# Transposing q and k by DMA instead of on TensorE, and score tiles in triples, in a fused attention and MLP kernel

## The chip, the cores and the metric

The kernel runs on one core of a Trainium2 chip. The metric is the device time of one execution in microseconds. The kernel before takes 482.68 us (median of 3 runs, 482.49 to 484.44).

## The reference, cut to what matters

```python
q_n, k_n = rmsnorm(q, g_q), rmsnorm(k, g_k)          # (8 batches, 12 heads, 448, 64)
scores = (1 / 8) * q_n @ k_n.T                       # per head
attn = softmax(scores); x = attn @ v                 # -> (3584, 768)
h = x @ w_in                                         # 768 -> 2048
out = (max(h, 0) + alpha * min(h, 0)) @ w_out        # 2048 -> 768
```

Inputs and output are float32; the kernel computes in float16 with float32 accumulation.

## The kernel before

Work goes by groups of four heads, three groups to a batch, 24 in all (numbered from 0). A group's q and k are loaded, squared (GpSimd), summed (DVE), given a reciprocal root (ACT) and scaled (GpSimd). Fourteen TensorE transposes, seven for q and seven for k, put them into PSUM, and DVE copies them out; the copy of k multiplies in both gains, so g_q and g_k enter there together. Scores are made in tiles: four 64x64 matmuls each, seven tiles to a group. An exponential on ACT follows. A group's denominators and value products are 28 matmuls each. The MLP of the batch before (128 up-projections, 56 down-projections in all) fills the gaps between bursts of score tiles.

```python
def turn(y):                                  # per group
    ps = psa.tile([128, 2, 512], FP32, name="tps", tag="acc")
    ...
    for tp, nm in zip(tps, "qk"):
        for j in range(J):                    # J = 7
            nc.tensor.transpose(tp[:, j, :], qs[y, nm][:, j]..., ident)
    for tp, nm in zip(tps, "qk"):
        t = att.tile([128, 2, J, 64], FP16, name=f"{nm}T", tag=f"{nm}T", bufs=3)
        if nm == "q": nc.vector.tensor_copy(out=o, in_=i4)
        else: nc.vector.tensor_scalar(out=o, in0=i4, scalar1=gain[:, 0:1], ..., op0=ALU.mult)
...
dens = {last(y) + 1: y for y in range(NG)}    # burst at which group y's denominators run
avs = {last(y) + 2: y for y in range(NG)}
...
for b in range(1, B):
    at(J * G * b / 2 - 4, load_v, b)          # v of batch 1 at burst 6
...
for c in range(4):
    load_w_in(c)                              # float32 -> float16, GpSimd's queue
    at(8 + 2 * c, load_w_out, c)
...
for n in range(NB + 2):                       # a burst: two score tiles
    ...
```

Of the kernel before, what the change touches and what calls it, by code (L numbers as in the profile page):

```python
# [21 lines left out]
def kernel(  # L22
# [51 lines left out]
    make_identity(nc, ident)  # L74
    idle = cst.tile([128, S], FP16, name="idle", tag="idle")
    nc.vector.memset(idle, 0.0)
    gain = cst.tile([128, 1], FP32, name="gain", tag="gain")
    gk2 = cst.tile([128, 1], FP32, name="gk2", tag="gk2")
    alpha_sb = cst.tile([128, NF], FP32, name="alpha_sb", tag="alpha_sb")
    w_in_sb = cst.tile([128, KM, DF], FP16, name="w_in_sb", tag="w_in_sb")  # L80
    w_out_sb = cst.tile([128, NF, DM], FP16, name="w_out_sb", tag="w_out_sb")
    gT = cst.tile([128, NF, W], FP16, name="gT", tag="gT")
# [2 lines left out]
    SRC = {"q": q4, "k": k4}  # L85


    def load_qk(y):
        b, i = divmod(y, G)
        for nm in "qk":  # L90
            t = ld.tile([128, 2, J, D], FP32, name="nat", tag="nat", bufs=6)
            for g in range(2):
                (nc.scalar if y < 2 and g else nc.sync).dma_start(
                    out=t[ds(64 * g, 64)].rearrange("p h j d -> p h (j d)"),
                    in_=SRC[nm][b, g, :, ds(2 * i, 2)],
                )
            nat[y, nm] = t
# [21 lines left out]

    def square(y, nm):  # L120
        src = nat[y, nm].rearrange("p h j d -> p (h j d)")
        sq = ld.tile([128, 2 * J, D], FP32, name="sq", tag="sq", bufs=2)
        sqf = sq.rearrange("p n d -> p (n d)")
        if y < 2:
            nc.scalar.activation(out=sqf, in_=src, func=AF.Square)  # L125
        else:
            nc.gpsimd.tensor_mul(out=sqf, in0=src, in1=src)  # L127
        sqs[y, nm] = sq
# [18 lines left out]
    def scale(y, nm):  # L147
# [6 lines left out]
        )  # L154
        qs[y, nm] = t

    def turn(y):

        ps = psa.tile([128, 2, 512], FP32, name="tps", tag="acc")
        tps = [  # L160
            ps[:, n, : S].bitcast(FP16).rearrange("p (j c) -> p j c", j=J)
            for n in range(2)
        ]
        for tp, nm in zip(tps, "qk"):
            for j in range(J):
                nc.tensor.transpose(  # L166
                    tp[:, j, :], qs[y, nm][:, j].rearrange("p h d -> p (h d)"), ident
                )
        for tp, nm in zip(tps, "qk"):
            t = att.tile([128, 2, J, 64], FP16, name=f"{nm}T", tag=f"{nm}T", bufs=3)  # L170
            o = t.rearrange("p g j c -> p j g c")
            i4 = tp.rearrange("p j (g c) -> p j g c", g=2)
            if nm == "q":
                nc.vector.tensor_copy(out=o, in_=i4)
            else:
                nc.vector.tensor_scalar(  # L176
                    out=o, in0=i4, scalar1=gain[:, 0:1], scalar2=None, op0=ALU.mult
                )
            qkT[y, nm] = t

# [3 lines left out]
    def score(y, j):  # L184
        qT, kT = qkT[y, "q"], qkT[y, "k"]
        sc = pss.tile([128, 2, 512], FP32, name="sc", tag="sc")
        for par in range(2):
            for g in range(2):
                nc.tensor.matmul(  # L189
                    out=sc[ds(64 * g, 64), par, :S],  # L190
                    lhsT=kT[ds(64 * par, 64), g, j, :],
                    rhs=qT[ds(64 * par, 64), g].rearrange("p j c -> p (j c)"),
                    start=True,
                    stop=True,
                )
        scs[y, j] = sc
# [33 lines left out]
    def invert(y):  # L230
        r = rden[y]
        nc.scalar.activation(out=r, in_=r, func=AF.Exp, scale=-1.0)  # L232
# [60 lines left out]



    NB = (NG * J + 1) // 2

    def last(y):
        return (J * y + J - 1) // 2

    dens = {last(y) + 1: y for y in range(NG)}
    avs = {last(y) + 2: y for y in range(NG)}
    prep, post, roots = {}, {}, {}

    def at(n, f, *a):
        prep.setdefault(max(int(n), 0), []).append((f, a))
# [1 line left out]
    def after(n, f, *a):  # L308
        post.setdefault(max(int(n), 0), []).append((f, a))

    turn_at = [J * y // 2 - 1 for y in range(NG)]
    turns = {n: y for y, n in enumerate(turn_at) if y}
    jobs = {}
    for y in range(G, NG):

        n = turn_at[y - 1] if y < G + 2 else last(y - G) + 2
        at(n - 8, load_qk, y)
        for nm in "qk":
            at(n - 2, square, y, nm)
            if y < G + 2:  # L320
                after(n, reduce, y, nm)
            else:
                jobs.setdefault(n, []).append((reduce, (y, nm)))
        roots[n + 1] = y
    for b in range(1, B):
        at(J * G * b / 2 - 4, load_v, b)


    UP, DOWN = 1.13, 2.6
# [2 lines left out]
    for b in range(B):  # L332
        ups = [(UP, up, (b, ft)) for ft in range(NF)]
        odd = b % 2
        new = [
            (DOWN, down, (b - odd, t, oh))
            for t in (range(3, J) if odd else range(3)) for oh in range(2)
        ]
        tail = len(new) if b == B - 1 else 2 + odd
        periods.append((ups, carry, new[:tail]))  # L340
        carry = new[tail:]

    def cost(n):
        return 0.75 + (1.35 if n in dens or n in avs else 0.0) + (0.9 if n in turns else 0.0)

    first = last(G - 1) + 2
    gaps = [[] for _ in range(NB + 2)]
    for b in range(B - 1):
        lo = last(G * b + G - 1) + 2
        hi = last(G * b + 2 * G - 1) + 2  # L350
        ups, old, new = (list(u) for u in periods[b])
        mlp = sum(u[0] for u in ups + old + new)
        per = (mlp + sum(cost(n) for n in range(lo, hi))) / (hi - lo)
        clock = 0.0
        for n in range(lo, hi):
            clock += cost(n)
            free = n in avs or n in turns
            while ups or old or new:
                if old and (free or not ups):
                    u = old.pop(0)  # L360
                elif ups:
                    u = ups.pop(0)
                else:
                    u = new.pop(0)
                gaps[n].append(u[1:])
                clock += u[0]
                free = False
                ahead = 0.5 * (UP if ups else DOWN)
                if n < hi - 1 and clock + ahead > per * (n - lo + 1):
                    break  # L370
    ups, old, new = periods[B - 1]
    rest = []
# [6 lines left out]

    load_qk(0)  # L380
    nc.scalar.preload_act_table_set("natural_log_exp_and_others")
    for g in range(2):
        nc.gpsimd.dma_start(out=gain[ds(64 * g, 64)], in_=g_q.unsqueeze(1))
        nc.gpsimd.dma_start(out=gk2[ds(64 * g, 64)], in_=g_k.unsqueeze(1))
    load_qk(1)
    load_qk(2)
    nc.sync.dma_start(out=alpha_sb, in_=moe_alpha.rearrange("(t p) -> p t", p=128))

    spin(34)
    for nm in "qk":  # L390
        square(0, nm)
        reduce(0, nm)
    for nm in "qk":
        root(0, nm)
        scale(0, nm)
    nc.vector.tensor_mul(out=gain, in0=gain, in1=gk2)
    turn(0)
    load_v(0)
    for y in (1, 2):
# [3 lines left out]
                reduce(y, nm)  # L403
    for c in range(4):
        load_w_in(c)
        at(8 + 2 * c, load_w_out, c)
    after(0, root, 1)
    for nm in "qk":
        after(0, scale, 1, nm)
        after(2, reduce, 2, nm)  # L410
    roots[3] = 2

    for n in range(NB + 2):
        for f, a in prep.get(n, ()):
            f(*a)
        tiles = [divmod(m, J) for m in (2 * n, 2 * n + 1) if m < NG * J]
        for t in tiles:
            score(*t)
        if n in dens:
            den(dens[n])  # L420
        if n in avs:
            attv(avs[n])

        plain = n not in dens and n not in avs and n not in turns
        wait = plain and gaps[n] and gaps[n][0][0] is up
        late = []
        for t in tiles[:1] if wait else tiles:
            soft(*t)
        if wait:
            late = [(1, soft, t) for t in tiles[1:]]  # L430
        if n in dens:
            log(dens[n])
            late = [(2, invert, (dens[n],))]
        if n in roots:
            y = roots[n]
            root(y)
            for nm in "qk":
                scale(y, nm)
        if n in turns:
            turn(turns[n])  # L440
        done = 0
        for f, a in gaps[n]:
            if f is down:
                down(*a, jobs.pop(n, ()))
            else:
                f(*a)
                done += 1
                if late and done == late[0][0]:
                    for _, g, c in late:
                        g(*c)  # L450
                    late = []
        for _, g, c in late:
            g(*c)
        if n < first:
            spin(4 if plain else 1)
        for f, a in jobs.pop(n, []) + post.get(n, []):
            f(*a)
    for f, a in rest:
# [31 lines left out]
```

## Time and profile before

| stretch (us) | PE busy | ACT | DVE | GpSimd | DMA engines |
|---|---|---|---|---|---|
| 40 to 65 | 21.1 of 25 | 20.5 | 12.2 | 17.0 | full |
| 65 to 100 | 33.5 of 35 | 25.2 | 19.4 | 15.9 | 0.56 |
| 100 to 400 | 292.0 of 300 | 192.2 | 141.3 | 107.8 | 0.33 |

From 100 us on PE has hardly anything left to wait for: time there is PE work. Up to the first up-projection PE runs idle matmuls to keep its clock up, and the end of the opening is set by loads, GpSimd, ACT and DVE. The prediction below shows the lines for both. It puts the first up-projection at 50.7 us; that is its third matmul. The first two stand at 49.39, and the third then waited 0.78 us for xT. Times of the first up-projection in the rest of this document are those of its first matmul, 49.39 before.

### The profile page before, as it was taken

What the parts mean: (1) busy time and instruction counts of PE and PEld (TensorE: products, weight loads), DVE (VectorE), ACT (ScalarE), POOL (GpSimd) and SP (SyncE); (2) the same over time, 40 slices, a digit from 0 to 9 for tenths busy, and PEclk for the clock granted to TensorE, in tenths of its full rate; (3) what the DMA queues carried; (4) which work ended last, traced back from release to release, by engine and by line L of the source; (5) the groups of instructions that cost most, each with busy time, mean ns of one, the idle gap of its engine ahead of it and who ended that gap; (6) DMA issues with size and microseconds to landing.
All of it is one profiled execution on the core that took longest, in us unless ns stands there. A gap on an engine that the chain in (4) does not pass through costs nothing.

```text
span 480.6 us, 9494 instructions
## 1 busy us (share of the span) xinstructions
PE 451.2 (94%) x4074; PEld 234.9 (49%) x4074; DVE 217.3 (45%) x312; ACT 289.1 (60%) x399; POOL 167.0 (35%) x123
## 2 busy tenths in 40 slices
PE   7777899999999999999999999999999999999995
PEld 3243444555455445555545554554545554555463
DVE  2843564545354445355453454454462443334421
ACT  4788789567756657656755757548674558423300
POOL 4688734554253261451442351532623200000000
PEclk9799999999999999999999999999999999999998
DMA  7999997340705243431704434423401110111122
GB/s 197 200 266 221 241 209 135 110 110 3 167 1 143 77 116 53 117 100 38 167 0 110 110 100 69 110 54 90 92 1 35 34 34 1 34 34 33 34 65 67
DMA packets 32187, 45.46 MB, mean 95 GB/s; under 512 B 5008, under 2 KB 28560, under 8 KB 32144
## 3 DMA queue, kind: packets, MB, share of 16 engines
q1 hardware_dynamic: 19792, 32.13, 25.8%
q0 software_dynamic: 11776, 11.80, 15.7%
q10 hardware_dynamic: 576, 0.92, 0.7%
q8 instruction: 32, 0.52, 0.5%
q14 instruction: 11, 0.09, 0.1%
HBM read 45.62 MB, written 11.01 MB: 118 GB/s over the span
## 4 chain that ended last, share of the span: by engine, by line
PE 70%; ACT 12%; DVE 9%; issue 4%; POOL 3%; DMA 1%; SPq 0%; POOLq 0%; DVEq 0%; ACTq 0%
PE op L266 30%; PE hT L249 20%; ACT ah L257 6%; PE sc L189 6%; PE av L212 6%; PE dn L212 4%; DVE gT L258 4%; ACT expT L201 4%; DVE ss L133 3%; PE tps L166 2%; DMA nat<-in_k_dram 1%; POOL qs L150 1%; POOL sq L127 1%; ACT rden L227 1%; PE spin L289 1%
## 5 line engine op out<-in xcount | busy, mean ns | idle before, releaser
L201 ACT ACTIVATE expT<-sc,expb 128x896 f16<-128x896 f32 x168 | 160.4, 1004 | 51.2 <-PE sc L189 51.1
L249 PE MATMUL hT<-xT,w_in_sb 128*128 128x448 f16 x768 | 159.9, 352 | 8.1 <-DVE gT L258 6.5
L266 PE MATMUL op<-w_out_sb,gT 128*128 128x384 f16 x896 | 153.3, 326 | 1.7 <-DVE gT L258 1.7
L257 ACT ACTIVATE ah<-hT,alpha_sb 128x448 f16<-128x448 f32 x128 | 80.7, 635 | 97.2 <-PE hT L249 96.2
L258 DVE TENSOR_TENSOR gT<-hT,ah 128x448 f16<-128x448 f32 x128 | 79.5, 624 | 123.5 <-ACT ah L257 123.3
L150 POOL TENSOR_TENSOR qs<-nat,rr 128x896 f16<-128x896 f32 x45 | 75.0, 1688 | 127.9 <-ACT rr L145 104.1
L266 PEld LDWEIGHTS <-gT 128*128 128x128 f16 x896 | 85.2, 98 | 64.3 <-issue 11.2
L249 PEld LDWEIGHTS <-w_in_sb 128*128 128x128 f16 x768 | 72.4, 97 | 86.0 <-issue 26.2
L127 POOL TENSOR_TENSOR sq<-nat 128x896 f32<-128x896 f32 x44 | 72.9, 1677 | 85.4 <-DVE ss L133 85.4
L278 DVE COPY osb<-op 128x384 f32<-128x384 f32 x56 | 31.1, 556 | 86.5 <-PE op L266 86.5
L189 PE MATMUL sc<-qT,kT 64*64 64x448 f16 x672 | 51.7, 370 | 9.9 <-DVE kT L176 4.5
L133 DVE TENSOR_REDUCE ss<-sq 128x14 f32<-128x896 f32 x48 | 49.8, 1076 | 7.0 <-ACT sq L125 7.0
L240 DVE TENSOR_TENSOR xT<-av,rden 128x896 f16<-128x896 f32 x24 | 26.2, 1092 | 29.9 <-PE av L212 29.9
L212 PE MATMUL av<-expT,vt 64*64 64x448 f16 x672 | 36.0, 349 | 1.3 <-ACT rden L227 1.3
L212 PE MATMUL dn<-expT,ones 64*64 64x448 f16 x672 | 35.9, 349 | 0.0
L189 PEld LDWEIGHTS <-kT 64*64 64x64 f16 x672 | 13.9, 105 | 42.7 <-issue 32.2
L212 PEld LDWEIGHTS <-vt 64*64 64x64 f16 x672 | 20.0, 107 | 13.6 <-issue 2.4
L212 PEld LDWEIGHTS <-ones 64*64 64x64 f16 x672 | 19.9, 107 | 11.8 <-issue 0.3
L166 PE MATMUL tps<-ident,qs 128*128 128x128 f16 x336 | 23.3, 220 | 1.9 <-POOL qs L150 1.6
L227 ACT ACTIVATE rden<-dn 128x896 f32<-128x896 f32 x24 | 22.1, 921 | 3.5 <-PE dn L212 3.5
L166 PEld LDWEIGHTS <-qs 128*128 128x128 f16 x336 | 18.8, 98 | 10.8 <-issue 5.6
L232 ACT ACTIVATE rden<-rden 128x896 f32<-128x896 f32 x24 | 22.6, 943 | 0.3
(25 smaller groups left out, 98.9 us busy)
## 6 DMA issues: line engine op xcount, KB each, us to landing
out_dram<-osb SPq DMA_DIRECT2D x56, 192.0 KB, 2.7
nat<-in_q_dram SPq DMA_DIRECT2D x46, 224.0 KB, 3.8
nat<-in_k_dram SPq DMA_DIRECT2D x46, 224.0 KB, 4.6
vt<-in_v_dram POOLq DMA_DIRECT2D x16, 336.0 KB, 5.5
w_in_sb<-in_moe_w_in_dram POOLq DMA_DIRECT2D x4, 768.0 KB, 19.0
w_out_sb<-in_moe_w_out_dram POOLq DMA_DIRECT2D x4, 768.0 KB, 16.2
nat<-in_q_dram ACTq DMA_DIRECT2D x2, 224.0 KB, 5.2
nat<-in_k_dram ACTq DMA_DIRECT2D x2, 224.0 KB, 7.1
```

The source lines that it names most:

```text
L127: nc.gpsimd.tensor_mul(out=sqf, in0=src, in1=src)
L133: nc.vector.tensor_reduce(out=ss_t[y][:, "qk".index(nm)].rearrange("p h j -> p (h j)").unsqueeze(2), in_=sqs[y, nm], axis=AXIS_X, op=ALU.add,)
L150: eng.tensor_mul(out=t.rearrange("p j h d -> p h j d"), in0=nat[y, nm], in1=rr_t[y][:, "qk".index(nm)].unsqueeze(3).broadcast_to((128, 2, ...
L166: nc.tensor.transpose(tp[:, j, :], qs[y, nm][:, j].rearrange("p h d -> p (h d)"), ident)
L189: nc.tensor.matmul(out=sc[ds(64 * g, 64), par, :S], lhsT=kT[ds(64 * par, 64), g, j, :], rhs=qT[ds(64 * par, 64), g].rearrange("p j c -> p ...
L201: nc.scalar.activation(out=expT[y][:, j], in_=scs[y, j][:, :, :S], func=AF.Exp, scale=QK_SCALE, bias=expb[:, 0:1],)
L212: nc.tensor.matmul(out=acc[ds(64 * par, 64), g, :S], lhsT=weights(g, par, j), rhs=e[ds(64 * g, 64), j, par, :], start=(j == 0), stop=(j == ...
L249: nc.tensor.matmul(out=hT[:, :S], lhsT=w_in_sb[:, c, ts(ft, 128)], rhs=x[:, c, :], start=(c == 0), stop=(c == KM - 1),)
L257: nc.scalar.activation(out=ah, in_=hT[:, :S], func=AF.Copy, scale=alpha_sb[:, ft : ft + 1])
L258: nc.vector.tensor_max(out=gT[:, ft, ds((b & 1) * S, S)], in0=hT[:, :S], in1=ah)
L266: nc.tensor.matmul(out=op[:, :OH], lhsT=gT[:, ft, ts(t, 128)], rhs=w_out_sb[:, ft, ds(oh * OH, OH)], start=(ft == 0), stop=(ft == NF - 1),)
L278: nc.vector.tensor_copy(out=o[:, ds(oh * OH, OH)], in_=op[:, :OH])
```

## The change

The intent: take 21 of 24 sets of transposes off the bounding engine. SP issues them as DMA transposes from SBUF to SBUF, and DVE multiplies the gain into k in place. The score tiles come in triples in bursts with denominators or value products, to switch TensorE's tiling less often. Around it: the layout of qT and kT, alpha and the gains loaded as rows and turned by one matmul, group 1's load held back, more buffers, other distances between loads and uses. Cut to its core:

```diff
+    def turn_dma(y):
+        for nm in "qk":
+            t = att.tile([128, J, 2, 64], FP16, name=f"{nm}T", tag=f"{nm}T", bufs=4)
+            nc.sync.dma_start(
+                out=t.rearrange("p j g c -> p j (g c)"),
+                in_=qs[y, nm].rearrange("p j h d -> p (j h d)"),
+                transpose=True,
+            )
+            qkT[y, nm] = t
     def turn(y):
+        if y >= G:                            # G = 3
+            t = qkT[y, "k"].rearrange("p j g c -> p (j g c)")
+            nc.vector.tensor_scalar(out=t, in0=t, scalar1=gain[:, 0:1], ..., op0=ALU.mult)
+            return
...
-                    rhs=qT[ds(64 * par, 64), g].rearrange("p j c -> p (j c)"),
+                    rhs=qT[ds(64 * par, 64), :, g, :],
...
+        wide = n in dens and dens[n] >= G or n in avs and avs[n] >= G - 1
+        count = min(3 if wide else 2, NG * J - m)
...
+        n = turn_at[y - 1] if early else max(d for d in dens if d <= turn_at[y] - 2)
...
-        at(J * G * b / 2 - 4, load_v, b)
+        at(av_at[G * b] - 4, load_v, b)
...
-        at(8 + 2 * c, load_w_out, c)
+        at(7 + c, load_w_out, c)
...
+            if y >= G:
+                turn_dma(y)                   # right after the scale
```

More of the change, by code (lines that the diff above doesn't have):

```diff
@@ L76 @@
     nc.vector.memset(idle, 0.0)
+    ident32 = cst.tile([32, 32], FP32, name="ident32", tag="ident32")
+    make_identity(nc, ident32)
+    rows = cst.tile([NF + 2, 128], FP32, name="rows", tag="rows")
+    cols = cst.tile([128, NF + 2], FP32, name="cols", tag="cols")
+    alpha_sb = cols[:, :NF]
     gain = cst.tile([128, 1], FP32, name="gain", tag="gain")
-    gk2 = cst.tile([128, 1], FP32, name="gk2", tag="gk2")
-    alpha_sb = cst.tile([128, NF], FP32, name="alpha_sb", tag="alpha_sb")
     w_in_sb = cst.tile([128, KM, DF], FP16, name="w_in_sb", tag="w_in_sb")
@@ L85, with load_qk @@
     SRC = {"q": q4, "k": k4}
-    def load_qk(y):
+    def load_qk(y, hold=False):
         b, i = divmod(y, G)
@@ L91, in load_qk @@
             t = ld.tile([128, 2, J, D], FP32, name="nat", tag="nat", bufs=6)
+            if hold and nm == "q":
+                nc.scalar.copy(out=t[:, 0, 0, 0:1], in_=expb)
             for g in range(2):
@@ L121, in square @@
         src = nat[y, nm].rearrange("p h j d -> p (h j d)")
-        sq = ld.tile([128, 2 * J, D], FP32, name="sq", tag="sq", bufs=2)
+        sq = ld.tile([128, 2 * J, D], FP32, name="sq", tag="sq", bufs=4)
         sqf = sq.rearrange("p n d -> p (n d)")
@@ L155, in scale @@
         qs[y, nm] = t
-    def turn(y):
+    def turn_dma(y):
[7 more added lines that the diff above has]
+            qkT[y, nm] = t
+    def turn(y):
+        if y >= G:
+            t = qkT[y, "k"].rearrange("p j g c -> p (j g c)")
+            nc.vector.tensor_scalar(
+                out=t, in0=t, scalar1=gain[:, 0:1], scalar2=None, op0=ALU.mult
+            )
+            return
         ps = psa.tile([128, 2, 512], FP32, name="tps", tag="acc")
+        ps2 = psf.tile([128, 512], FP32, name="tps2", tag="mm") if y == 0 else ps[:, 1]
         tps = [
-            ps[:, n, : S].bitcast(FP16).rearrange("p (j c) -> p j c", j=J)
-            for n in range(2)
+            t[:, : S].bitcast(FP16).rearrange("p (j c) -> p j c", j=J)
+            for t in (ps[:, 0], ps2)
         ]
@@ L169, in turn @@
         for tp, nm in zip(tps, "qk"):
-            t = att.tile([128, 2, J, 64], FP16, name=f"{nm}T", tag=f"{nm}T", bufs=3)
-            o = t.rearrange("p g j c -> p j g c")
-            i4 = tp.rearrange("p j (g c) -> p j g c", g=2)
+            t = att.tile([128, J, 2, 64], FP16, name=f"{nm}T", tag=f"{nm}T", bufs=4)
+            o = t.rearrange("p j g c -> p j (g c)")
             if nm == "q":
-                nc.vector.tensor_copy(out=o, in_=i4)
+                nc.vector.tensor_copy(out=o, in_=tp)
             else:
                 nc.vector.tensor_scalar(
-                    out=o, in0=i4, scalar1=gain[:, 0:1], scalar2=None, op0=ALU.mult
+                    out=o, in0=tp, scalar1=gain[:, 0:1], scalar2=None, op0=ALU.mult
                 )
@@ L189, in score @@
                 nc.tensor.matmul(
-                    out=sc[ds(64 * g, 64), par, :S],
-                    lhsT=kT[ds(64 * par, 64), g, j, :],
-                    rhs=qT[ds(64 * par, 64), g].rearrange("p j c -> p (j c)"),
+                    out=sc[ds(64 * g, 64), par, :S].rearrange("p (j c) -> p j c", j=J),
+                    lhsT=kT[ds(64 * par, 64), j, g, :],
+                    rhs=qT[ds(64 * par, 64), :, g, :],
                     start=True,
@@ L291, in spin @@
                 )
-    NB = (NG * J + 1) // 2
-    def last(y):
-        return (J * y + J - 1) // 2
-    dens = {last(y) + 1: y for y in range(NG)}
-    avs = {last(y) + 2: y for y in range(NG)}
+    bursts, dens, avs, first_in, last_in = [], {}, {}, {}, {}
+    m = 0
+    while m < NG * J or len(avs) < NG:
+        n = len(bursts)
+        if len(dens) > len(avs):
+            avs[n] = len(avs)
+        elif len(dens) < NG and last_in.get(len(dens), n) < n:
+            dens[n] = len(dens)
+        wide = n in dens and dens[n] >= G or n in avs and avs[n] >= G - 1
+        count = min(3 if wide else 2, NG * J - m)
+        bursts.append([divmod(m + c, J) for c in range(count)])
+        for y, j in bursts[n]:
+            first_in.setdefault(y, n)
+            if j == J - 1:
+                last_in[y] = n
+        m += count
+    NB = len(bursts)
+    den_at = {y: n for n, y in dens.items()}
+    av_at = {y: n for n, y in avs.items()}
     prep, post, roots = {}, {}, {}
@@ L309, in after @@
         post.setdefault(max(int(n), 0), []).append((f, a))
-    turn_at = [J * y // 2 - 1 for y in range(NG)]
-    turns = {n: y for y, n in enumerate(turn_at) if y}
+    turn_at = {
+        y: max(n for n in range(first_in[y]) if n not in dens) for y in range(1, NG)
+    }
+    turns = {n: y for y, n in turn_at.items()}
     jobs = {}
     for y in range(G, NG):
-        n = turn_at[y - 1] if y < G + 2 else last(y - G) + 2
-        at(n - 8, load_qk, y)
+        early = y < G + 2
+        n = turn_at[y - 1] if early else max(d for d in dens if d <= turn_at[y] - 2)
+        at(n - (8 if early else 5), load_qk, y)
         for nm in "qk":
             at(n - 2, square, y, nm)
-            if y < G + 2:
+            if early:
                 after(n, reduce, y, nm)
@@ L338 @@
         ]
-        tail = len(new) if b == B - 1 else 2 + odd
+        tail = len(new) if b == B - 1 else 2 if odd or b == 0 else 1
         periods.append((ups, carry, new[:tail]))
@@ L343, in cost @@
     def cost(n):
-        return 0.75 + (1.35 if n in dens or n in avs else 0.0) + (0.9 if n in turns else 0.0)
-    first = last(G - 1) + 2
-    gaps = [[] for _ in range(NB + 2)]
+        return (
+            0.31 + 0.19 * len(bursts[n])
+            + (1.35 if n in dens or n in avs else 0.0) + (0.9 if turns.get(n, G) < G else 0.0)
+        )
+    first = av_at[G - 1]
+    gaps = [[] for _ in range(NB)]
     for b in range(B - 1):
-        lo = last(G * b + G - 1) + 2
-        hi = last(G * b + 2 * G - 1) + 2
+        lo, hi = av_at[G * b + G - 1], av_at[G * b + 2 * G - 1]
         ups, old, new = (list(u) for u in periods[b])
@@ L356 @@
             clock += cost(n)
-            free = n in avs or n in turns
+            free = True
             while ups or old or new:
@@ L368 @@
                 ahead = 0.5 * (UP if ups else DOWN)
-                if n < hi - 1 and clock + ahead > per * (n - lo + 1):
+                short = n in turns and len(gaps[n]) < 2
+                if n < hi - 1 and not short and clock + ahead > per * (n - lo + 1):
                     break
@@ L381 @@
     nc.scalar.preload_act_table_set("natural_log_exp_and_others")
-    for g in range(2):
-        nc.gpsimd.dma_start(out=gain[ds(64 * g, 64)], in_=g_q.unsqueeze(1))
-        nc.gpsimd.dma_start(out=gk2[ds(64 * g, 64)], in_=g_k.unsqueeze(1))
-    load_qk(1)
+    nc.gpsimd.dma_start(out=rows[:NF], in_=moe_alpha.rearrange("(t p) -> t p", p=128))
+    for n, g in enumerate((g_q, g_k)):
+        for h in range(2):
+            nc.gpsimd.dma_start(
+                out=rows[NF + n : NF + n + 1, ds(64 * h, 64)], in_=g.unsqueeze(0)
+            )
+    load_qk(1, True)
     load_qk(2)
-    nc.sync.dma_start(out=alpha_sb, in_=moe_alpha.rearrange("(t p) -> p t", p=128))
-    spin(34)
+    spin(22)
+    ct = psf.tile([128, 512], FP32, name="ct", tag="mm")
+    nc.tensor.transpose(ct[:, : NF + 2], rows, ident32[: NF + 2, : NF + 2])
+    spin(12)
     for nm in "qk":
@@ L392 @@
         reduce(0, nm)
-    for nm in "qk":
         root(0, nm)
         scale(0, nm)
-    nc.vector.tensor_mul(out=gain, in0=gain, in1=gk2)
+        if nm == "q":
+            nc.vector.tensor_copy(out=cols, in_=ct[:, : NF + 2])
+            nc.vector.tensor_mul(
+                out=gain, in0=cols[:, NF : NF + 1], in1=cols[:, NF + 1 : NF + 2]
+            )
     turn(0)
@@ L411 @@
     roots[3] = 2
-    for n in range(NB + 2):
+    for n in range(NB):
         for f, a in prep.get(n, ()):
             f(*a)
-        tiles = [divmod(m, J) for m in (2 * n, 2 * n + 1) if m < NG * J]
-        for t in tiles:
+        tiles = bursts[n]
+        for t in tiles[:2]:
             score(*t)
+        plain = n not in dens and n not in avs
+        wait = plain and gaps[n] and gaps[n][0][0] is up
+        for t in tiles[:1] if wait else tiles[:2]:
+            soft(*t)
         if n in dens:
@@ L422 @@
             attv(avs[n])
-        plain = n not in dens and n not in avs and n not in turns
-        wait = plain and gaps[n] and gaps[n][0][0] is up
+        for t in tiles[2:]:
+            score(*t)
+            soft(*t)
         late = []
-        for t in tiles[:1] if wait else tiles:
-            soft(*t)
         if wait:
@@ L432 @@
             log(dens[n])
-            late = [(2, invert, (dens[n],))]
+            if gaps[n] and gaps[n][0][0] is down:
+                invert(dens[n])
+            else:
+                late = [(1, invert, (dens[n],))]
         if n in roots:
@@ L438 @@
                 scale(y, nm)
-        if n in turns:
-            turn(turns[n])
+            if y >= G:
+                turn_dma(y)
         done = 0
-        for f, a in gaps[n]:
+        for k, (f, a) in enumerate(gaps[n]):
             if f is down:
@@ L451 @@
                     late = []
+            if k == 0 and n in turns:
+                turn(turns[n])
+        if not gaps[n] and n in turns:
+            turn(turns[n])
         for _, g, c in late:
@@ L454 @@
         if n < first:
-            spin(4 if plain else 1)
+            spin(4)
         for f, a in jobs.pop(n, []) + post.get(n, []):
```

## The prediction

> **What bounds the kernel now.** I read the page's engine totals, then the busy time in equal stretches, the waits of PE, a timeline of one turn in the steady part, and last the transfers of the first 65 us. The totals and slices:
>
> ```profile
> PE 451.2 (94%) x4074; PEld 234.9 (49%) x4074; DVE 217.3 (45%) x312; ACT 289.1 (60%) x399; POOL 167.0 (35%) x123
> ...
> PE   7777899999999999999999999999999999999995
> ...
> PEclk9799999999999999999999999999999999999998
> DMA  7999997340705243431704434423401110111122
> ```
>
> PE is busy almost everywhere except the first five slices (12 us each), at full clock. All other engines are below two thirds. Summing the six stretches from 100 to 400 us gives PE 292.0 of 300: nothing but PE work can be taken away there. The waits of PE say the same:
>
> ```profile
> PE hT L249 <- DVE gT L258: 6.5, 25, 0.3
> PE sc L189 <- DVE kT L176: 4.5, 5, 1.3
> PE sc L189 <- ACT ah L257: 2.9, 5, 0.8
> PE sc L189 <- ACT expT L201: 2.4, 5, 0.5
> PE op L266 <- DVE gT L258: 1.7, 6, 0.3
> ```
>
> Columns: total us, times, longest. In 480.6 us no single wait exceeds 7 us, and the five waits for kT lie in the first 45 us. The 8.2 us for gT are pieces of about 0.25, one wherever two up-projections run in a row and the third unit needs the first one's PSUM buffer.
>
> A turn of the steady part, PE alone (start, length, what):
>
> ```profile
> 203.94 2.77 PE L266 MATMUL op<-w_out_sb,gT 128*128 128x384 f16 x16
> 206.64 0.57 PE L189 MATMUL sc<-qT,kT 64*64 64x448 f16 x8
> 207.15 0.96 PE L166 MATMUL tps<-ident,qs 128*128 128x128 f16 x14
> 207.94 2.76 PE L266 MATMUL op<-w_out_sb,gT 128*128 128x384 f16 x16
> ...
> 217.61 0.57 PE L189 MATMUL sc<-qT,kT 64*64 64x448 f16 x8
> 218.02 1.49 PE L212 MATMUL dn<-expT,ones 64*64 64x448 f16 x28
> 219.44 2.44 PE L249 MATMUL hT<-xT,w_in_sb 128*128 128x448 f16 x12
> ```
>
> I measure from start to start, since the lengths overlap. Fourteen transposes hold PE for 207.94 - 207.15 = 0.79 us. Two score tiles hold it 0.51 us if 128-row work follows and 0.41 if the denominators follow.
>
> The first 50.7 us, until the first up-projection, are different: PE fills time with idle matmuls, and the chain runs through the k load, DVE, GpSimd and ACT. There the DMA engines are full:
>
> ```profile
> DMA packets 8350, 10.77 MB, mean 239 GB/s; under 512 B 457, under 2 KB 8345, under 8 KB 8345
> ```
>
> That is 20 to 65 us. A q or k load takes a median 7.2 or 8.3 us to land there, against 3.8 and 4.6 over the whole run, because the two weight matrices stream in at the same time.
>
> **What the skill says.** The Trainium skill, "TensorE: Matmul & The Clock Gate", Part 4, says a TensorE transpose goes to PSUM and needs a Vector copy after it, and gives some 275 ns in a kernel. The trace has 219 ns for one, but 14 in 0.79 us, 56 ns apart, so the cost on the path is far below the latency. "TensorEngine Tiling (Array Packing)", Key Properties, says that changing the tiling mode drains TensorE; 0.51 against 0.41 us agrees. "DMA: Bandwidth & Descriptors", Latency and other measured facts, gives DMA transpose 261 GB/s with a non-contiguous middle dimension; no transfer of that kind is in the trace before, so this is the weakest number here. "VectorE: DVE Perf Modes", Mode 4x_2P, says 16-bit single-source operations from SBUF to SBUF can do four elements a cycle; the trace has only PSUM sources (0.62 and 0.68 us for 896 columns), so it cannot confirm it.
>
> **The change, part by part.**
>
> (a) Transposes leave PE. Of 24 sets three stay on PE. In the instruction order, 20 sets stand after the first up-projection before the change and none after it: 20 x 0.79 = 15.8 us off the bounding engine. The set of the fourth group lies in the opening, where PE is not the bound.
>
> (b) Triples. Counting from the first up-projection, PE goes from 128-row work to 64-row work and back 73 times before and 53 times after. One visit costs 0.51 - 0.41 = 0.10, plus about 0.02 on entry (the up-projection ahead of a score takes 1.23 instead of 1.215): 20 x 0.12 = 2.4 us. The third tile stands behind the denominators or the value product, so it reuses their visit; it needs the PSUM buffer of the first tile, whose exponential ends about 1.65 us after the scores start in the burst at 217.61, while the 28 matmuls end at 1.83: about no wait.
>
> (c) DVE. 21 q copies of 0.622 go, and 21 k multiplies of 0.675 become SBUF to SBUF. Estimate by the Vector page: 896/4/0.96 GHz = 0.23, with start-up 0.3 us. DVE loses 21 x (0.622 + 0.675 - 0.3) = 21 us of 217, off the path. The 0.25 us waits for gT are a round of ACT and DVE; the pattern that makes them occurs 41 times before and 40 after. I count 0.5 us.
>
> (d) Start. The alpha and gain loads become rows, turned by one PE transpose, and group 1's load is held until ACT has run a copy after its table load (3.4 us). Group 0's k landed at 8.3 us beside 2.7 MB of other loads; with them held back I estimate 6.8. The first kT follows: 1.5 us gained.
>
> (e) The opening's fourth group pays. Its scale runs on GpSimd from about 34.5 us (three earlier than before, since the square buffers double and GpSimd need not wait for DVE). The k transpose is issued at 38, has to share full DMA engines, and like the loads there takes some 7 us: 45. Its score stood at 42.7 and would now want 41. I count 3 us (some of it absorbed).
>
> (f) ACT comes in lumps. A burst with denominators now has three exponentials of 0.95 us, not two, ahead of the log and the next up-projection's prelu: 0.95 - 0.19 = 0.76 us more lag. Where three or more up-projections follow it, PE waits. Some four or five places: 3 us. This is a choice, not a measurement.
>
> Sum: -15.8 - 2.4 - 0.5 - 1.5 + 3 + 3 = -14.2, so 482.7 - 14.2 = 468.5, say 468.
>
> **Rivals.** *The transposes land late.* From a group's root to its multiply lie two or three bursts. 52 bursts over about 345 us make 6.6 us a burst, so two bursts and the first up-projection give 17 us. The root runs some 5 us into its burst (three exponentials, the log), GpSimd needs 2 x 1.69, and the second transpose can start at 8.3. That leaves 8 to 9 us for both. A plain load of the same size lands in 3.2 at best; 229 kB at 261 GB/s is 0.9 us plus some 2.3 of latency, so both in about 5. It fits if a transpose takes under 4.5 us or so. If each takes 9, half the groups (those with two bursts) are about 7 us late, DVE holds gT behind the multiply in its queue, PE runs out of PSUM and the time becomes about 468 + 10 x 7 = 540. Nothing in the trace before rules it out; that the distance was set to at least two bursts speaks against.
>
> *ACT takes over.* ACT's 289 us do not change, and 289/468 is 62%; with lumps at every one of 21 denominators costing 0.76 us it would be 13 us more than I count: 478, within 2%. For it: 2.9 + 2.4 us of PE waits on ACT already. Against: the schedule places a down-projection (2.7 us of PE and no ACT) first in most of those bursts.
>
> *The opening takes back more.* If the transposes of groups 3 and 4 wait out the weight streams, whose issues move earlier by one to four bursts, the first up-projection slips by 8 rather than 3 us: 473, on the edge of 2%.
>
> **Range and chances.** The removed PE work is sure and worth 3.8%; what is added can eat a third of it by small lags, or all of it by slow transposes. Everything going well (no 3 + 3) is 462, with a denser mix 457; the ACT rival and the opening together reach 484. So 457 to 484. The 2% line is 473.0. Faster 0.70; the same 0.18, if two of the three losses are larger than I count; slower 0.12, nearly all the late-transpose case.
>
> **What would show it.** PE busy near 430 with no transposes past the third group, and the waits for gT still near 8 us, confirm (a) to (c). The transposes' time from issue to landing decides the first rival: under 5 us right, over 8 wrong; then PE waits for hT by gT and DVE waits for DMA at kT would stand out. The first up-projection should start near 52 us; past 57 makes (e) wrong. PE waits on ACT (expT, ah, or gT through ah) above 15 us would make (f) wrong. A score of two tiles that takes more than 0.51 us start to start would mean that the now strided q operand slows the matmul, which I took to be free.

## The result and the profile after

The changed kernel takes 482.25 us (median of 4 runs, 481.97 to 482.45), before 483.04 in the same rounds. The ratio is 0.9979, with a 95% interval from 0.9956 to 1.0002: no difference.

The page's engine totals and slices of the changed kernel:

```profile
PE 433.6 (90%) x3805; PEld 227.2 (47%) x3805; DVE 205.5 (43%) x292; ACT 289.5 (60%) x400; POOL 170.6 (36%) x126
...
PE   7792179789998999999999999999999999999995
...
PEclk9997588999999999999999999999999999999999
DMA  8999988359561982585645646737317311011122
```

PE's busy time fell by 17.6 us, as it should. The span did not: slices four and five (36 to 60 us) say 2 and 1 tenths of PE, where the kernel before had 7 and 8, and the clock fell to 5 in the fifth. DMA stays full there. PE's waits and DVE's longest wait for a DMA, of the changed kernel (total us, times, longest):

```profile
PE sc L212 <- DVE kT L178: 24.3, 4, 18.8
DVE kT L178 <- DMA kT<-qs: 21.0, 2, 20.2
...
PE hT L272 <- DVE gT L281: 7.9, 21, 1.0
PE sc L212 <- ACT expT L224: 2.6, 6, 0.8
...
PE op L289 <- DVE gT L281: 0.5, 2, 0.2
```

One wait carries it: 18.8 us, for the kT of one group, which DVE could not multiply because its DMA had not landed. The timeline of PE places it, first before, then changed:

```profile
42.74 0.38 PE L189 MATMUL sc<-qT,kT 64*64 64x448 f16 x4 [0.81 <-DVE kT L176]
...
49.39 0.55 PE L249 MATMUL hT<-xT,w_in_sb 128*128 128x448 f16 x2
```

```profile
39.10 0.38 PE L212 MATMUL sc<-qT,kT 64*64 64x448 f16 x4
58.24 0.59 PE L212 MATMUL sc<-qT,kT 64*64 64x448 f16 x4 [18.76 <-DVE kT L178]
...
66.84 0.55 PE L272 MATMUL hT<-xT,w_in_sb 128*128 128x448 f16 x2
```

It is group 3, the first on the DMA path, in the burst in which the kernel before made the same score tile at 42.74. The first up-projection comes at 66.84 instead of 49.39: 17.5 us late. From there to the end the changed kernel takes 480.5 - 66.8 = 413.7 us, the kernel before 480.6 - 49.4 = 431.2: 17.5 us less. Gain and loss cancel.

The chain of waits from 25 to 75 us (start, length, what):

```profile
36.98 0.88 POOL qs L157
37.86 0.75 issue
38.61 0.07 POOL w_out_sb L121
38.68 19.03 DMA kT<-qs
57.71 0.02 issue
57.74 0.45 DVE kT L178
```

The k transpose was issued at 38.68, which is where I expected it, and took 19.03 us to land. Over the whole run such a transfer is quick (count, median us from issue to landing):

```profile
qT<-qs SPq DMA_TRANSPOSE x21, 2.9
kT<-qs SPq DMA_TRANSPOSE x21, 4.1
```

So the question is why it took 19 us there. The DMA queues from 44 to 50 us (packets, MB, share of the engines' time; q0 is GpSimd's queue with the weights, q1 is SP's):

```profile
q0 software_dynamic: 701, 1.04, 94.4%
q1 hardware_dynamic: 703, 0.17, 22.0%
```

The two queues moved the same number of packets, but the transposes' are small. From 38 to 44 us, where SP's queue held only the two transposes, its 345 packets carried 0.09 MB, 256 bytes each; a weight packet in the 44 to 50 window carries 1.04 MB / 701 = 1.5 kB. Over the run the change added 36,942 packets and 9.61 MB for 42 transposes, 880 packets and 229 kB each, so a transpose is 896 packets of 256 bytes, a few records missing. If queues take turns packet by packet, the two transposes of a group need 2 x 896 / 16 = 112 turns on each engine. In 44 to 50 us each engine made 701 / 16 = 44 turns in 6 us, 0.137 us a turn: 15 us for a group as long as the weights stream. That is theory A.

Measured, group 3's k landed 20.7 us after its q was issued (37.03 to 57.71), and the trace shows two parts. From 37 to 41 us SP's queue moved 5 packets while GpSimd's moved 810: the transposes, though issued, had not begun. From 41 to 57 us the counts are even, 1850 and 1857, and nearly all of SP's packets are the transposes' 2 x 896. So theory A describes the last 16 us; why SP's queue stood still for the first 3.9 stays open. It did so in copy_3 below as well, for 3.8 us.

The steady part looks as predicted (PE, changed kernel):

```profile
208.34 0.57 PE L212 MATMUL sc<-qT,kT 64*64 64x448 f16 x8
208.74 1.49 PE L235 MATMUL dn<-expT,ones 64*64 64x448 f16 x28
210.06 0.36 PE L212 MATMUL sc<-qT,kT 64*64 64x448 f16 x4
210.35 1.31 PE L272 MATMUL hT<-xT,w_in_sb 128*128 128x448 f16 x6
```

The third score tile follows the denominators without a wait, the strided q operand costs nothing (two tiles still take 0.40 us start to start), and no transposes stand in PE's way.

### The profile page after: what moved, and what is told of

Read it like the earlier page. It is cut to its first block, busy times and chain, and to the rows that moved or that the text cites. A ratio compares the mean times of both kernels' runs of the same rounds, so it can differ in the third digit from the quotient of the medians.

```text
span 480.5 us, 9024 instructions
## 1 busy us (share of the span) xinstructions
PE 433.6 (90%) x3805; PEld 227.2 (47%) x3805; DVE 205.5 (43%) x292; ACT 289.5 (60%) x400; POOL 170.6 (36%) x126
## 4 chain that ended last, share of the span: by engine, by line
PE 68%; ACT 12%; DMA 8%; DVE 6%; issue 3%; POOL 2%; SPq 0%; POOLq 0%; ACTq 0%
PE op L289 31%; PE hT L272 21%; PE sc L212 6%; ACT expT L224 6%; DMA kT<-qs 5%; PE dn L235 5%; PE av L235 4%; ACT ah L280 4%; DVE gT L281 4%; DMA nat<-in_k_dram 2%; DVE kT L178 1%; POOL qs L157 1%; DMA rows<-in_g_k_dram 1%; DVE ss L140 1%; ACT rden L250 1%
## 5 line engine op out<-in xcount | busy, mean ns | idle before, releaser
L224 ACT ACTIVATE expT<-sc,expb 128x896 f16<-128x896 f32 x168 | 157.7, 1007 | 33.6 <-PE sc L212 33.4
L280 ACT ACTIVATE ah<-hT,cols 128x448 f16<-128x448 f32 x128 | 81.1, 634 | 121.3 <-PE hT L272 121.1
L157 POOL TENSOR_TENSOR qs<-nat,rr 128x896 f16<-128x896 f32 x45 | 77.7, 1746 | 199.6 <-issue 157.8
L272 PEld LDWEIGHTS <-w_in_sb 128*128 128x128 f16 x768 | 74.0, 98 | 84.1 <-issue 22.5
L212 PE MATMUL sc<-qT,kT 64*64 64x448 f16 x672 | 53.5, 363 | 28.8 <-DVE kT L178 24.3
L212 PEld LDWEIGHTS <-kT 64*64 64x64 f16 x672 | 18.5, 105 | 59.6 <-issue 27.0
L235 PE MATMUL dn<-expT,ones 64*64 64x448 f16 x672 | 36.9, 356 | 0.0
L178 DVE TENSOR_SCALAR kT<-kT,gain 128x896 f16<-128x896 f16 x21 | 14.9, 708 | 21.0 <-DMA kT<-qs 21.0
L312 PE MATMUL spin<-idle,ident 128*128 128x448 f16 x82 | 20.5, 392 | 1.4 <-POOL ident masks.py:197 1.4
```

The costliest lines, as they stand in the source:

```text
L157: eng.tensor_mul(out=t.rearrange("p j h d -> p h j d"), in0=nat[y, nm], in1=rr_t[y][:, "qk".index(nm)].unsqueeze(3).broadcast_to((128, 2, ...
L212: nc.tensor.matmul(out=sc[ds(64 * g, 64), par, :S].rearrange("p (j c) -> p j c", j=J), lhsT=kT[ds(64 * par, 64), j, g, :], rhs=qT[ds(64 * ...
L224: nc.scalar.activation(out=expT[y][:, j], in_=scs[y, j][:, :, :S], func=AF.Exp, scale=QK_SCALE, bias=expb[:, 0:1],)
L235: nc.tensor.matmul(out=acc[ds(64 * par, 64), g, :S], lhsT=weights(g, par, j), rhs=e[ds(64 * g, 64), j, par, :], start=(j == 0), stop=(j == ...
L272: nc.tensor.matmul(out=hT[:, :S], lhsT=w_in_sb[:, c, ts(ft, 128)], rhs=x[:, c, :], start=(c == 0), stop=(c == KM - 1),)
L280: nc.scalar.activation(out=ah, in_=hT[:, :S], func=AF.Copy, scale=alpha_sb[:, ft : ft + 1])
```

## The experiments

All edits are to the changed kernel. Theory A is the one above. Rival B: any 229 kB takes long where the engines are full, whatever its packets. Rival C: the first DMA transpose of a kernel is slow for a reason of its own.

**pe_to_3, pe_to_4**: groups up to 3, or up to 4, go back to TensorE.

```diff
-        if y >= G:                     # in turn
+        if y >= 4:                     # pe_to_4: 5
...
-            if y >= G:
+            if y >= 4:                 # pe_to_4: 5
                 turn_dma(y)
```

The same threshold is moved in `cost`, an estimate by which the schedule places MLP work between the bursts; this holds for every run with a threshold.

> Group 3's two transposes go back to TensorE, groups 4 to 23 stay on DMA. Theory A (packet turns): a transpose is cut into 256-byte packets that take turns one for one with the weight stream's packets of some 1.2 KB, so a pair of transposes needs about 15 us for as long as weights stream (until about 58 us). The 18.8 us wait of PE goes; group 4's transposes are issued at about 45 us, land only when the stream ends, and PE waits some 5 us for them: 471 us. Rival B (bytes): any transfer of 229 kB needs 7 to 8 us there, group 4 then lands in time: 466 us. Rival C (the first crossbar transpose of a kernel is slow, or it waits for something of its own): the wait of 18 us moves to group 4: 482 us.

> Groups 3 and 4 back on TensorE, groups 5 to 23 on DMA. Theory A: no transpose meets the weight stream in a place where PE needs it soon; PE waits for kT under 2 us in all, first up-projection at about 49 us, 466 us (482.3 less the 18.8 and 2.6 us waits, plus what the cold clock cost, less some absorbed). Rival B: the same. Rival C: an 18 us wait at group 5, 480 us or more.

pe_to_3 took 475.74 us (ratio 0.9853, 0.9832 to 0.9873), pe_to_4 467.99 (0.969, 0.9667 to 0.9712); both correct. In pe_to_3 PE waited 15.1 us for group 4, more than the 5 that I expected from A and close to C: the k transpose took 17.9 us, because the second batch's v was queued behind the weights and kept GpSimd's queue busy beyond 58 us. The first up-projection had been made by then (48.0 us). In pe_to_4 group 5's transposes are the first ones, and no 18 us wait moved to them. That alone doesn't rule out C: the k transpose still needed 13.9 us, but had landed by 69.5 us, and DVE did not multiply before 75.34. The 2.1 us that PE waited there went with the multiply, 1.93 us long. But a new wait stands in the list of pe_to_4:

```profile
PE av L235 <- DMA vt<-in_v_dram: 4.6, 2, 2.9
```

The value product waits for v, whose load this change had moved from burst 6 to burst 11, behind all four w_out loads in GpSimd's queue. In the changed kernel the long wait had hidden that.

**late_w_out**: the weights out of the way of group 3.

```diff
-        at(7 + c, load_w_out, c)
+        at(12 + c, load_w_out, c)
```

> All transposes as in the changed kernel; only the four w_out loads are issued at bursts 12 to 15 instead of 7 to 10. Theory A: with the stream gone, group 3's k transpose lands in about 5 us instead of 19 and PE waits under 3 us for it; group 5's transposes, issued at about 54 us, now meet the stream and take 15 us, but have about that much slack: 468 us, up to 475 if they or the first down-projection come late. Rival B: the same, 466. Rival C: the wait of 18 us stays, 482.

474.89 us (0.984, 0.9807 to 0.9873), correct. The wait for group 3 fell from 18.8 to 5.5 us (the k transpose was issued at 38.72, and DVE had it at 44.51, 5.8 us later), so the traffic beside it was the cause, not the transpose: this rules out C. I had expected under 3 us of wait. It is a poor remedy: later groups meet the weights instead, and PE waited 3.8, 3.3 and 1.3 us for them, 13.9 in all. That is why the time is at the upper end of what I had written.

**copy_3 and copy_3_256**: wrong results. Group 3's two DMAs become plain copies of the same bytes between the same tiles, first in whole rows of 1792 bytes, then, by padding the source rows, in pieces of 256 bytes. This separates theory A from B, and from the idea that the transposing as such suffers.

```diff
-                transpose=True,
+                **({} if y == G else {"transpose": True}),
```
```diff
 # copy_3_256, as well:
+        if y == G:
+            t = ld.tile([128, J, 3, D], FP16, name="qs", tag="qs3", bufs=2)[:, :, 0:2]
 # and the DMA's source is then taken as "p j (h d)": 7 pieces of 256 bytes a row
```

> Wrong result on purpose: group 3's two DMAs copy the same bytes between the same tiles without transposing, in rows of 1792 bytes. Theory A: 128 packets each instead of 896, so they take few turns and land in 3 to 5 us beside the same weight stream; the wait of 18.8 us shrinks to under 3, and group 4's transposes then meet the stream, 471 us. Rival B (bytes, or the engines' load as such): they land in about the same 12 to 19 us as the transposes did, 482 us.

> Wrong result on purpose: as copy_3, but the source rows are padded so that the plain copy has to go in pieces of 256 bytes, 896 of them as a transpose has. Theory A (packet turns): it lands like the transposes, 12 us and more for q and up to 19 for k, and PE waits some 15 to 19 us at group 3. Rival (the crossbar transpose as such is what suffers beside other traffic): it lands like copy_3, about 6 us, and PE waits about 6.

One run each: copy_3 479.4 us, copy_3_256 481.87, both of unknown state, so only the traces count. From issue to landing, copy_3:

```profile
qT<-qs SPq DMA_DIRECT2D x1, 224.0 KB, 5.9
kT<-qs SPq DMA_DIRECT2D x1, 224.0 KB, 6.1
```

copy_3_256:

```profile
qT<-qs SPq DMA_DIRECT2D x1, 224.0 KB, 12.5
kT<-qs SPq DMA_DIRECT2D x1, 224.0 KB, 18.7
```

The transposes had taken 12.7 and 19.0. The same bytes in pieces of 256 bytes land as late as the transposes do, and in pieces of 1792 bytes in a third to a half of the time. So transposing costs nothing extra here and the byte count is not the cause: the packet size is. PE's wait for group 3 was 5.8 us in copy_3, where I had expected under 3, and 18.4 in copy_3_256. From the first packet on, the pair took 3.9 us in copy_3 (41.57 to 45.5) and some 16 in copy_3_256 (41.03 to 57.4); the standstill before it is the same in both. The queues from 44 to 50 us agree; copy_3, whose SP queue by then held q and k loads in 1792-byte rows:

```profile
q0 software_dynamic: 517, 0.77, 70.0%
q1 hardware_dynamic: 515, 0.82, 42.5%
```

copy_3_256:

```profile
q0 software_dynamic: 692, 1.04, 94.2%
q1 hardware_dynamic: 694, 0.17, 22.0%
```

In both, packets are shared one for one in this window; with the large rows SP's queue gets half of the bytes, with the small pieces a seventh. In copy_3 the delay moves on: group 4's transposes then met the stream, and PE waited 11.4 us for them, where I had expected about 5.

**pe_to_5, pe_all, pairs_dma5**: how far to go back, and what each part is worth alone.

```diff
 # pe_to_5: threshold 6;  pe_all: threshold NG;  pairs_dma5: threshold 5 and
-        wide = n in dens and dens[n] >= G or n in avs and avs[n] >= G - 1
+        wide = False
```

> Groups 3 to 5 back on TensorE. If in pe_to_4 the transposes of group 5, which took 13.9 us beside the weights, also held back what queues with them (v of the second batch: 4.6 us of PE waits; kT of group 5: 2.1 us), both waits shrink: 468.0 less 6.7 plus 0.8 for one more set on TensorE, 463 us. If v is late because of the weights alone, only the 2.1 go: 467 us.

> No DMA transposes at all: triples, the new start and the buffers alone. By the sum in the prediction: 19 sets x 0.79 = 15.0 us more PE work than in pe_to_4, less the 6.7 us of its waits: 476 us. If removed PE time does not come back one for one, nearer 468.

> As pe_to_4 (DMA transposes from group 5 on), but score tiles in pairs throughout. By the prediction's visit cost, 20 more visits x 0.12 = 2.4 us: 470.4 us. If triples cost more in lumps on ACT than they save, 466 or less.

pe_to_5 took 468.24 us (0.9699, 0.9682 to 0.9715), not 463: the wait for v stayed, at 5.5 us, so it was late from its place in the queue and not from the transposes of group 5. pe_all took 485.20 (1.0056, 1.004 to 1.0071) where I had written 476. My expectation had subtracted waits that pe_all has as well: PE waited 5.7 us for v there too.

pairs_dma5 took 505.65 us (1.047, 1.0442 to 1.0497), far from 470. Its waits:

```profile
DVE kT L178 <- DMA kT<-qs: 33.9, 16, 5.2
...
PE hT L272 <- DVE gT L281: 21.7, 31, 4.2
```

This is the chain of the prediction's rival "transposes land late", but here each transpose landed quickly (a median of 2.9 us for q and for k) and was asked for too soon. With pairs, the rule "denominators at least two bursts before the multiply" leaves one burst between root and multiply, against two or three with triples. The multiply stands in DVE's queue waiting for the DMA, gT waits behind it, and PE waits for gT to free hT's buffer in PSUM. Under this rule the two halves of the change depend on each other; pairs_far_v below changes the rule.

**v_early, v_early_5, pe_all_v, pairs_far_v**: v of the second batch back at burst 6, ahead of w_out.

```diff
-        at(av_at[G * b] - 4, load_v, b)
+        at(6 if b == 1 else av_at[G * b] - 4, load_v, b)
 # thresholds: v_early 5, v_early_5 6, pe_all_v NG, pairs_far_v 5 and
+        wide = False
-        n = ... max(d for d in dens if d <= turn_at[y] - 2)
+        n = ... max(d for d in dens if d <= turn_at[y] - 3)
```

> pe_to_4 with v of the second batch loaded at burst 6, ahead of the w_out loads, as the kernel before has it, instead of behind all four. In pe_to_4 that v was issued at 47.6 us and PE waited 4.6 us for it in two pieces, after which its clock had dropped (0.90 in the stretch 65 to 100). Theory: the wait and the cold clock, some 2.5 us, go: 468.0 - 7 = 461 us. Rival: w_out, now later by one v, moves the wait to the first down-projection, or group 5's transposes take its place: 466 to 468.

> As v_early with group 5 on TensorE too. Its transposes were the last to meet the weights (13.9 us) and cost PE 2.1 us; one more set on TensorE costs 0.8. Expected 0 to 1.5 us less than v_early: 460 us; the same as v_early if the 2.1 us are absorbed elsewhere.

> All sets on TensorE, triples, new start, v early: what is left of the change without any DMA transpose. Against pe_all (485.2) the 5.7 us wait for v and its cold clock go: 477 us. Against the kernel before (482.8) this is then what triples (2.4 predicted) and the opening (2.7 us earlier first up-projection) bring: 477.7. If triples bring nothing, 480.

> As v_early, but pairs instead of triples, and the root of each group one set of denominators earlier, so that the DMA transposes have at least two bursts as in the triples. In pairs_dma5 one burst of some 5 us was left, and DVE waited 33.9 us for the transposes. Theory: the 505.7 us came from that distance alone; with it restored only the 20 more visits x 0.12 = 2.4 us are left: v_early + 2.4, 463 us. Rival: pairs themselves are bad beside DMA transposes (SP's queue, ACT order): 480 us or more.

All four give correct results. I had expected 461, 460, 477.7 and 463 us; the last was missed by 7. (The 2.7 us in the expectation of pe_all_v count from 50.72, the third matmul of the first up-projection, as the prediction does.) v_early took 462.95 us (0.9595, 0.9573 to 0.9617), v_early_5 461.69 (0.9562, 0.9544 to 0.9581), pe_all_v 478.94 (0.9921, 0.9902 to 0.994), pairs_far_v 470.04 (0.9733, 0.9709 to 0.9758). From pairs_dma5 to pairs_far_v it is 35.6 us, of which v early brought 5 to 7 in the other pairs of runs; most of the rest goes with the longer distance. v_early_5 is the fastest kernel, 4.4% under the kernel before. In it the first up-projection stands at 48.48 us, and its largest waits of PE are small:

```profile
PE hT L272 <- DVE gT L281: 8.1, 21, 1.0
PE sc L212 <- DVE kT L199: 2.5, 6, 0.8
PE sc L212 <- ACT expT L224: 1.8, 5, 0.6
```

In v_early the waits for v are gone, 5.0 us better than pe_to_4; group 5's k came late instead and PE waited 4.3 us for it, so part of the rival in my expectation held. Taking group 5 off the DMA as well removed most of that and gave 1.3 us.

From pe_all_v to v_early_5 only the path of 18 sets differs (and with it what `cost` says of their bursts): 478.94 - 461.69 = 17.25 us, 0.96 us a set. PE's busy time differs by 448.9 - 433.6 = 15.3, 0.85 a set; the rest fits smaller waits (PE waited for DVE 3.4 us before transposes and 2.8 before down-projections with all sets on PE, against 1.1 and 0.7).

For the triples there are two measures, and they do not agree. pe_all_v against the kernel before is 3.8 us, of which the earlier first up-projection (48.47 against 49.39) is 0.9, or 1.7 with the 0.78 us wait inside it that is gone; this leaves 2.1 to 2.9 for triples and everything else that changed after the opening. v_early against pairs_far_v is 7.1 us, but that pair also has four or five bursts between root and multiply instead of two or three, and 11.0 us of waits for gT against 8.9. What triples alone are worth is not settled; both signs are positive.

## Why the prediction was wrong

The mechanism and the main terms were right; one term of the sum was mis-sized by a factor of six, and it cancelled the gain.

*(a) Transposes leave PE*: right. Predicted 15.8 us for 20 sets, 0.79 each; measured 0.96 each over 18 sets, of which 0.85 is PE's busy time and the rest waits that go with them.

*(b) Triples*: predicted 2.4; between 2.1 and 7.1 by two comparisons that do not isolate it. The third tile waits for nothing, as predicted. What I missed is that triples also make the distance which lets the transposes land.

*(c) DVE*: small, as counted, but the step "with start-up 0.3 us" was off. The in-place multiply took 0.44 to 1.69 us, median 0.66, so DVE lost 217.3 - 205.5 = 11.8 us, not 21. It lies off the path. The 0.3 left out most of a fixed cost: the cycle table of the cited page (the Trainium skill, "VectorE: DVE Perf Modes", Side-by-side) adds some 150 cycles to each instruction, and with 8 to fill the pipe an estimate from it is (896/4 + 158) / 0.96 GHz = 0.40 us. The two multiplies of the changed kernel with no GpSimd instruction beside them took 0.44 and 0.45 us, near that; the other nineteen, each beside one, took 0.47 to 1.69.

*(d) Start*: right in direction, too large at first. The square of group 0's k began at 7.86 instead of 8.38 us, and the first score at 13.85 instead of 14.42: 0.6 us, not 1.5. The square no longer waited for its load but stood behind ACT's root of q (7.41 to 7.95). By the first up-projection, with nothing late, the opening is 0.9 us shorter, or 1.7 with the wait that is gone (pe_all_v).

*(e) The opening's fourth group*: this step failed. "The k transpose is issued at 38, has to share full DMA engines, and like the loads there takes some 7 us: 45" treated the transpose as a load of the same bytes. The issue time was right (38.68); the landing took 19.0 us, and PE waited 18.8 instead of 3. A load there has 1792-byte rows and a transpose 256-byte packets, and from 41 us on the queues took turns by packet. The Trainium skill states this arbitration in "DMA: Bandwidth & Descriptors", Queues, rings and completion order: each engine round-robins between queues "at *packet* granularity". The prediction drew no number from it. The equal counts in the trace agree; but the page's packet is a bundle ("≈9-17 descriptors typical"), and whether it holds one or several of the pieces that the trace counts as packets no run here shows. The profile before gave one half of what was needed: 8350 packets and 10.77 MB from 20 to 65 us are 1.3 kB a packet. The transpose's packet size was in no trace before, and the size of the loss hung on it. copy_3 shows that my 7 us was about right for large rows (6.1). The standstill up to 41 us (2.3 of k's 19.0 us, 2.2 of the 6.1) was in no step of the prediction.

*(f) ACT in lumps*: did not happen. PE waited 2.6 us for ACT before scores (5.3 before the change) and 8.4 for gT (8.2 before). The 3 us were over-counted.

The sum after the first up-projection was good: -15.8 - 2.4 - 0.5 + 3 = -15.7, measured -17.5. Some of that is luck: 20 sets at 0.96 are 19.2 us, not 15.8, and PE lost 5.6 us in three more waits for kT between 70 and 104 us, which no term had. The opening was +17.5 instead of the +1.5 of (d) and (e).

*The rivals.* "The opening takes back more" was the right one, named with 8 us where it was 17.5, and the reason given (weight streams) was right. "Transposes land late" in the steady part was wrong for this kernel (2.9 and 4.1 us to land, under my 4.5). With pairs its chain came about, through a shorter distance and not through late landing. "ACT takes over" was wrong. The test that I had set, a first up-projection past 57 us, told against (e) at once: it stood at 66.84.

What stays open is the triples' own share and the standstill of SP's queue before 41 us.

## What to carry to other kernels

When a transfer has to share full DMA engines with another queue's stream, count its packets, not its bytes: here the time was packets per engine (112) times the time of a turn (some 0.14 us, in which the other queue's packet went too), after up to 4 us in which nothing moved. By these runs, use a transfer in small packets only where its consumer is many microseconds away or nothing else streams, and leave the first few uses, under the weight loads, on an engine. After a large wait has been removed, look at the waits again: here it had hidden a load that the same change had put behind the weights, worth another 5 to 7 us.

## What the Trainium skill lacked or had wrong

- "DMA: Bandwidth & Descriptors", Why small descriptors are slow (HBM only), says that "SBUF↔SBUF transfers don't suffer this penalty". The penalty meant there is a cost per packet, and no run here measures it. What that place lacks is that small packets cost such a transfer its share beside another queue's stream: the same 229 kB from SBUF to SBUF landed in 5.9 and 6.1 us in pieces of 1792 bytes, and in 12.5 and 18.7 us in pieces of 256 (copy_3, copy_3_256).
- The same page gives the turns by packet, and its table of what the engines do besides copying names a "256B-tile transpose"; no page says that an SBUF-to-SBUF transpose takes its turns in packets of that size, or what this means for its share. Here they carried 256 bytes: 703 packets with 0.17 MB against 701 with 1.04 MB of weights in 6 us. The page's 261 GB/s does not tell the time beside a stream: over the run a q transpose of 229 kB landed in a median of 2.9 us; in the stream, q's took 12.7 and k's 19.0.
- No page says how long a queue's first packet can wait beside another queue's stream: here 3.9 us from the issue of the q transpose.
